# Dummy matmuls from a preset constant and re-queued first loads at the start of an attention-plus-GLU kernel

## The chip, the cores and the metric

The kernel runs on one core of a Trainium2 chip. The time is the device time of one execution in microseconds (us); "span" is the time from the first to the last instruction in the trace, about 1.7 us less. Every kernel here is timed next to the kernel before, on the same chip, in the same rounds.

## The reference

```python
xn = layernorm(x)                                  # x: 1 x 2048 x 512, bf16
q, k, v = split_heads(xn @ wqkv)                   # 32 heads of 16
phi(a) = concat(softmax(a @ w_phi), softmax(-(a @ w_phi)))
o = phi(q) @ (phi(k)^T v) / (phi(q) @ sum(phi(k)) + 1e-6)
out = x + o @ wo + ((xn @ w_gate) * (xn @ w_up)) @ w_down      # inner width 1792
```

Tokens are handled in 16 tiles of 128. What matters here is the start: load x tiles 0 to 3, centre and transpose them, multiply tiles 0 and 1 by the v weights, run the first two gate/up units, then fold `w_phi` into the k weights. From there on TensorE never waits.

## The kernel before

The first loads go out on two queues, SyncE's (SP) and ScalarE's (ACT), in this order (one load fetches one *slice* of a weight matrix, or one or two tiles of x):

```python
    load_x(0, 1)                 # SP : x tile 0, 128 KB
    load_x(1, 1, ACT)            # ACT: x tile 1
    load_v(SP, 0)                # first half of the v weights, 256 KB
    load_v(ACT, 1)               # second half
    load_x(2, 2)                 # tiles 2 and 3, 256 KB
    load_gu(ACT, 0, (0,))        # first gate slice, 256 KB
    load_gu(SP, 0, (1,))         # first up slice
    load_gu(SP, 1)               # next slices
    ...
    dve(lambda e: e.memset(zero, 0.0), [], ["zero"], 256)
```

TensorE's program starts with dummies on those zeros, which only keep the array busy:

```python
    def warm(n, w=512):
        def fn(e):
            ...
            for _ in range(n):
                ins = e.matmul(bank(7, 0, w), lhsT=zero[:, 0:128], rhs=zero[:, 0:w], start=True, stop=True)
            return ins
        sc.step(PE, fn, ["zero"], [("ps", 7)], n * w * 0.8)

    warm(7)
    ...                              # statistics, centring
    x_transpose(0, 2, 0, 2)
    x_transpose(0, 3, 1, 2)
    warm(2, 128)
    v_matmul(0, 0, (0,))
    x_transpose(1, 4, 0, 2, DVE)
    x_transpose(1, 5, 1, 2, DVE)
    v_matmul(0, 0, (1,))
    v_matmul(1, 1)
    ...
    g0a()                            # first halves (256 tokens) of two gate/up units
    g1a()
    x_transpose(2, 2)
    u0a()
    x_transpose(3, 3)
    u1a()
    ...
    g0b()                            # second halves: need tiles 2 and 3
```

Steps of one engine run in program order; a step waits on semaphores for the data that it reads. A load waits for nothing.

The softmax here doesn't subtract the row's maximum and nothing guards it: scores larger than these inputs give would overflow.

## Time and profile before

| | before |
|---|---|
| median, lowest, highest of the first three runs | 222.69, 222.11, 223.19 us |
| span of the profiled run (223.13 us) | 221.4 us |
| TensorE share of the chain that ended last | 96% |
| first real matmul work (transpose of tile 0) | 4.88 us |
| first fold of `w_phi` | 15.50 us |

The first fold is my marker for the whole start, because behind it TensorE runs without a wait: a later fold is a longer run by nearly the same amount (from first fold to the end of the span it is 205.83 to 205.90 us in all fourteen traces).

The timeline of TensorE in the kernel before; the columns are start and duration in us, engine, line, operation, output and input, shape of weights and moving operand, count, and in brackets the idle time before and what ended it. Neighbours of one line are merged, so durations overlap and a line can hold more than one shape.

```profile
1.25 3.17 PE L644 MATMUL ps<-arena 128*128 128x512 bf16 x7 [1.25 <-DVE arena L296]
4.88 0.61 PE L421 MATMUL ps<-arena 128*128 128x128 bf16 x4 [0.47 <-DVE arena L389]
...
5.76 1.04 PE L223 MATMUL ps<-arena 128*128 128x512 bf16 x2
6.59 0.63 PE L421 MATMUL ps<-arena 128*128 128x128 bf16 x4
7.01 3.43 PE L223 MATMUL ps<-arena 128*128 128x512 bf16 x14
10.28 0.39 PE L421 MATMUL ps<-arena 128*128 128x128 bf16 x4
...
12.02 3.65 PE L223 MATMUL ps<-arena 128*128 128x256 bf16 x24 [0.25 <-ACT arena L204]
15.50 0.61 PE L337 MATMUL ps<-arena 128*128 128x128 bf16 x8
```

L644 is the dummies, L421 the transposes, L223 the v and gate/up matmuls, L337 the fold. TensorE idles before the first transpose, and once more before 12.02, where the second halves wait for ScalarE to copy tile 3's transpose out of PSUM, the memory that TensorE writes to. (Matmul ends are modelled. By the starts of the matmuls the second gap is 0.42 us longer than the spacing that they should have.)

How fast the array runs is read from groups by shape. This is the group of the eight v matmuls in 5.5 to 9.45 us of the kernel before (count, busy us, mean ns of one, idle before):

```profile
L223 PE MATMUL ps<-arena 128*128 128x512 bf16 x8 | 3.6, 605 | 0.1
```

One takes 605 ns here and 379 ns in the steady part. Starts of neighbours lie 0.427 us apart up to 9.15 us; afterwards two of 256 columns take 0.218: half rate, then full. I call that change the *release* of the clock; it is at 9.2 here. The loads of ScalarE's queue:

```profile
0.79 1.28 ACT L759 ACT_TABLE_LOAD   x1 [0.79 <-PEq L887]
0.82 0.39 ACTq L249 DMA_DIRECT2D arena<-in_A_x_dram  x1
1.25 0.46 ACTq L260 DMA_DIRECT2D arena<-in_A_wqkv_dram  x1
1.74 0.50 ACTq L260 DMA_DIRECT2D arena<-in_B_w_gate_dram  x1
```

Landings (last of the 16 completion records of each load): tile 0 at 3.57, tile 1 3.73, v halves 5.43 and 5.72, tiles 2/3 7.17, first gate slice 8.56, first up slice 8.78.

### The profile page before, as it was taken

The page shows a single profiled execution, that of the slowest core. Times are in us where ns is not written, and L with a number is a line of the kernel's source. Part 1 is how long each engine was busy: PE and PEld are TensorE (multiplying, and loading weights), DVE is VectorE, ACT ScalarE, POOL GpSimd, SP SyncE. Part 2 cuts the span into 40 slices and gives each one's busy share as a digit, 9 for nine tenths or more (in the row PEclk, how much of TensorE's full clock was granted, in tenths as well). Part 3 has the DMA queues.
Part 4 walks back from the last instruction along what each step waited for, and adds up shares of the span by engine and source line. Part 5 has one row for each costly group of instructions (what it writes and reads, how often), then busy time and mean ns, then how long its engine had stood idle before and what let it go on. Part 6 is the DMA issues. An engine that isn't in the chain of part 4 may idle for free.

```text
span 221.4 us, 3319 instructions
## 1 busy us (share of the span) xinstructions
PE 217.0 (98%) x1275; PEld 105.9 (48%) x1275; DVE 141.5 (64%) x246; ACT 85.8 (39%) x161; POOL 53.4 (24%) x119
## 2 busy tenths in 40 slices
PE   6999999999999999999999999999999999999995
PEld 2565444444444454444444444544445444444453
DVE  3646899887466655674586565697776677545341
ACT  4268964687524543444346435531112221000000
POOL 3030273331222012201232422225342222200000
DMA  5998627299200000000002211244674445352221
GB/s 175 280 313 279 150 94 131 58 291 231 47 3 0 0 0 3 0 0 0 3 0 47 49 25 25 51 82 84 149 159 98 109 105 116 76 118 73 60 63 47
DMA packets 47248, 19.90 MB, mean 90 GB/s; under 512 B 37504, under 2 KB 46720, under 8 KB 47232
## 3 DMA queue, kind: packets, MB, share of 16 engines
q1 hardware_dynamic: 46288, 19.03, 35.3%
q10 hardware_dynamic: 944, 0.66, 0.9%
q8 instruction: 10, 0.16, 0.3%
q14 instruction: 6, 0.05, 0.1%
HBM read 8.67 MB, written 2.10 MB: 49 GB/s over the span
## 4 chain that ended last, share of the span: by engine, by line
PE 96%; DMA 1%; DVE 1%; ACT 0%; issue 0%
PE ps L223 91%; PE ps L543 2%; PE ps L496 2%; DMA arena<-in_A_x_dram 1%; PE ps L337 1%; PE ps L421 1%; ACT arena L204 0%; DVE arena L364 0%; DVE arena L389 0%; DVE arena L625 0%; DVE arena L365 0%
## 5 line engine op out<-in xcount | busy, mean ns | idle before, releaser
L223 PE MATMUL ps<-arena 128*128 128x512 bf16 (+3 forms) x962 | 208.9, 373 | 0.3 <-ACT arena L204 0.3
L223 PEld LDWEIGHTS ps<-arena 128*128 128x128 bf16 x962 | 91.2, 98 | 99.3 <-ACT arena L204 0.8
L204 ACT ACTIVATE arena<-ps 128x512 bf16<-128x512 f32 (+2 forms) x114 | 63.0, 593 | 89.3 <-PE ps L223 74.6
L601 DVE TENSOR_TENSOR arena<-ps,arena 128x512 bf16<-128x512 f32 x56 | 38.5, 687 | 23.3 <-PE ps L223 18.0
L451 DVE TENSOR_REDUCE arena<-arena 128x64 f32<-128x1024 bf16 x32 | 38.5, 1214 | 21.0 <-ACT arena L204 21.0
L461 POOL TENSOR_TENSOR arena<-arena 128x512 bf16<-128x512 bf16 x32 | 33.8, 1056 | 1.3
L459 POOL TENSOR_TENSOR arena<-arena 128x32 f32<-128x32 f32 x32 | 8.5, 267 | 91.2 <-DVE arena L455 50.8
L625 DVE TENSOR_TENSOR arena<-ps,arena 128x512 bf16<-128x512 f32 (+2 forms) x13 | 8.5, 650 | 21.5 <-PE ps L223 21.5
L204 ACT ACTIVATE arena<-arena 128x512 bf16<-128x512 bf16 (+2 forms) x28 | 14.2, 519 | 5.7 <-DMA arena<-in_A_x_dram 2.9
L204 ACT ACTIVATE arena<-ps,arena 128x512 bf16<-128x512 f32 x16 | 10.1, 685 | 5.7 <-PE ps L223 5.7
L364 DVE BATCH_NORM_STATS2 arena<-arena 128x6 f32<-128x512 bf16 x16 | 10.4, 672 | 2.4 <-DMA arena<-in_A_x_dram 2.4
L564 DVE TENSOR_TENSOR arena<-ps,arena 128x512 bf16<-128x512 f32 x16 | 11.1, 691 | 0.5
L484 DVE TENSOR_TENSOR arena<-ps,arena 128x512 bf16<-128x512 f32 x16 | 10.3, 643 | 0.0
L455 DVE RECIPROCAL arena<-arena 128x64 f32<-128x64 f32 x16 | 8.4, 533 | 0.0
L496 PEld LDWEIGHTS ps<-arena 128*128 128x128 bf16 x128 | 6.2, 97 | 3.8
L543 PEld LDWEIGHTS ps<-arena 128*128 128x128 bf16 x128 | 6.2, 97 | 3.8
L401 POOL TENSOR_SCALAR arena<-arena 128x1 f32<-128x1 f32 x12 | 3.0, 265 | 19.1 <-ACT arena L204 19.1
L543 PE MATMUL ps<-arena 128*128 128x68 bf16 x128 | 6.7, 194 | 0.0
L496 PE MATMUL ps<-arena 128*128 128x68 bf16 x128 | 6.7, 194 | 0.0
L563 DVE RECIPROCAL arena<-arena 128x32 f32<-128x32 f32 x16 | 5.7, 353 | 0.6
L457 DVE RECIPROCAL arena<-arena 128x32 f32<-128x32 f32 x16 | 5.4, 344 | 0.2
L478 POOL CAST arena<-arena 128x32 bf16<-128x32 f32 x16 | 5.1, 321 | 0.0
(31 smaller groups left out, 35.1 us busy)
## 6 DMA issues: line engine op xcount, KB each, us to landing
out_dram<-arena SPq DMA_DIRECT2D x15, 128.0 KB, 1.7
arena<-in_B_w_down_dram SPq DMA_DIRECT2D x1, 1792.0 KB, 8.0
arena<-in_A_x_dram SPq DMA_DIRECT2D x3, 512.0 KB, 3.8
arena<-arena SPq DMA_TRANSPOSE x44, 2.6
arena<-in_B_w_gate_dram SPq DMA_DIRECT2D x1, 640.0 KB, 8.4
arena<-in_B_w_up_dram SPq DMA_DIRECT2D x1, 640.0 KB, 9.5
arena<-in_B_w_gate_dram SPq DMA_DIRECT2D x1, 512.0 KB, 5.1
arena<-in_B_w_up_dram SPq DMA_DIRECT2D x1, 512.0 KB, 6.1
```

The lines of the kernel that those rows point to most:

```text
L204: return sc.step(ACT, lambda e: e.activation(out=out_ap, in_=in_ap, func=func, scale=scale, **kw), reads, writes, 130.0 + 0.833 * n)
L223: ins = e.matmul(out_ap, lhsT=l, rhs=r, start=start and i == 0, stop=stop and i == npair - 1, **kw)
L364: dve(lambda e: e.bn_stats(stats_v[:, t, 0:6], x_tile(t)), [("x", t)], [("st", t)], 512)
L451: dve(lambda e: e.tensor_reduce(out=sm, in_=e_v, axis=AX.X, op=ALU.add), [(name, s, 0), (name, s, 1)], [("sums", sr)], 1024)
L459: pool(lambda e: e.tensor_tensor(out=rat, in0=sm[:, :, 0], in1=rs[:, :, 1], op=ALU.mult), [("sums", sr), ("rs", s)], [("rat", s)], 32)
L461: pool(lambda e: e.tensor_tensor(out=e_v[:, :, 1, :], in0=e_v[:, :, 1, :], in1=rat[:, :, None].to_broadcast([128, H, 16]), op=ALU.mult), [ ...
L484: dve(lambda e: e.tensor_tensor(out=vs_tile(t)[:, :, 0:16], in0=bank(b).rearrange("p (h f) -> p h f", h=H), in1=rp.unsqueeze(2).to_broadca ...
L496: ins = e.matmul(bank(c // 4, (c % 4) * CW, CW), lhsT=ek[:, c * 128:(c + 1) * 128], rhs=vs[:, c * CW:(c + 1) * CW], start=(t == 0 and c % ...
L543: ins = e.matmul(bank(b0 + c // 4, (c % 4) * CW, CW), lhsT=ph[:, c, :], rhs=kvz_v[:, c, :], start=True, stop=True)
L564: dve(lambda e: e.tensor_tensor(out=o_tile(t).rearrange("p (b h f) -> p b h f", b=2, f=16), in0=nd[:, :, :, 0:16], in1=w_v[:, r].unsqueeze ...
L601: dve(lambda e: e.tensor_tensor(out=hT_v[:, ft, sg * 512:(sg + 1) * 512], in0=bank(bu), in1=g, op=ALU.mult), [("ps", bu), ("g", s)], [("hT ...
L625: dve(lambda e, ps=ps, stg=stg, cs=cs: e.tensor_tensor(out=stg, in0=ps, in1=x_tile(t)[:, cs], op=ALU.add), [("ps", bk), ("x", t)], [("ostg ...
```

## The change

The intent: (1) dummies on a constant that the framework has already written when the engines are released, so that they start about 0.45 us earlier; (2) tiles 0 and 1 in one load with nothing beside it, because the second queue is to begin only behind ScalarE's table load (a small activation, `pace`, stands ahead of its loads); (3) the transposes of tiles 2 and 3 one gate/up part earlier, so that their copies finish in time. Cut to its core:

```diff
-    load_x(0, 1)
-    load_x(1, 1, ACT)
+    load_x(0, 2)
     load_v(SP, 0)
-    load_v(ACT, 1)
-    load_x(2, 2)
-    load_gu(ACT, 0, (0,))
-    load_gu(SP, 0, (1,))
+    load_v(SP, 1)
+    load_gu(SP, 0, (0,))
+    act(sbf("lnv", 0, 1), eps_f, ["eps"], ["pace"])
+    load_x(2, 2, ACT)
+    load_gu(ACT, 0, (1,))
     load_gu(SP, 1)
...
-    dve(lambda e: e.memset(zero, 0.0), [], ["zero"], 256)
...
-                ins = e.matmul(bank(7, 0, w), lhsT=zero[:, 0:128], rhs=zero[:, 0:w], start=True, stop=True)
+                ins = e.matmul(bank(7, 0, w), lhsT=nc.const_aps.tensor(1.0, (128, 128), BF16),
+                               rhs=nc.const_aps.tensor(1.0, (128, w), BF16), start=True, stop=True)
...
-    warm(7)
+    warm(8)
+    warm(1, 256)
...
-    warm(2, 128)
-    v_matmul(0, 0, (0,))
+    warm(1, 128)
     x_transpose(1, 4, 0, 2, DVE)
     x_transpose(1, 5, 1, 2, DVE)
-    v_matmul(0, 0, (1,))
+    v_matmul(0, 0)
     v_matmul(1, 1)
...
     g0a()
+    x_transpose(2, 2)
     g1a()
-    x_transpose(2, 2)
+    x_transpose(3, 3)
     u0a()
-    x_transpose(3, 3)
     u1a()
```

More of the change, by code (lines that the diff above doesn't have):

```diff
@@ L150, in _build @@
     alloc("ostg", 3 * 512)
-    alloc("zero", 512, at=layout["hT"])
     alloc("wphi", NQ * 16)
@@ L231, in _build @@
     mask = sb("mask", 0, CW)
-    zero = sb("zero", 0, 512)
     eps_f = sbf("eps", 0, 1)
@@ L276, in load_v, with c_fn @@
         load_w(eng, wv_v[:, 2 * h:2 * h + 2, :], i, ("wv", h), 262144)
+    def c_fn(e):
+        e.memset(ident, 0.0)
+        e.memset(mask16, 1.0)
+        return e.memset(mask, 1.0)
+    pool(lambda e: e.memset(eps_f, 1e-5), [], ["eps"], 1)
+    pool(c_fn, [], ["const"], 300)
     sc.pin = True
-    load_x(0, 1)
-    load_x(1, 1, ACT)
+    load_x(0, 2)
     load_v(SP, 0)
-    load_v(ACT, 1)
-    load_x(2, 2)
-    load_gu(ACT, 0, (0,))
-    load_gu(SP, 0, (1,))
+    load_v(SP, 1)
[3 more added lines that the diff above has]
+    load_gu(ACT, 0, (1,))
     load_gu(SP, 1)
@@ L293, in _build @@
     sc.pin = False
-    dve(lambda e: e.memset(zero, 0.0), [], ["zero"], 256)
-    def c_fn(e):
-        e.memset(ident, 0.0)
-        e.memset(mask16, 1.0)
-        e.memset(mask, 1.0)
-        return e.memset(eps_f, 1e-5)
-    pool(c_fn, [], ["const", "eps"], 300)
     def select(ap, op, fill, base, pattern, cm):
@@ L601, in gate @@
         dve(lambda e: e.tensor_tensor(out=hT_v[:, ft, sg * 512:(sg + 1) * 512], in0=bank(bu), in1=g, op=ALU.mult),
-            [("ps", bu), ("g", s)], [("hT", ft, sg)] + (["zero"] if ft == 0 and sg == 0 else []), 512)
+            [("ps", bu), ("g", s)], [("hT", ft, sg)], 512)
         sc.prio = 1
@@ L643, in fn @@
             for _ in range(n):
-                ins = e.matmul(bank(7, 0, w), lhsT=zero[:, 0:128], rhs=zero[:, 0:w], start=True, stop=True)
-            return ins
-        sc.step(PE, fn, ["zero"], [("ps", 7)], n * w * 0.8)
-    warm(7)
+                ins = e.matmul(bank(7, 0, w), lhsT=nc.const_aps.tensor(1.0, (128, 128), BF16),
+                               rhs=nc.const_aps.tensor(1.0, (128, w), BF16), start=True, stop=True)
+            return ins
+        sc.step(PE, fn, [], [("ps", 7)], n * w * 0.8)
+    warm(8)
+    warm(1, 256)
     sc.pin = True
```

## The prediction

> **What bounds the kernel now.** TensorE. The chain of waits gives PE 96% of the 221.4 us span and shows no PE wait after 12.02 us. The change leaves that part alone. Only the first 12 us can move. The timeline of that stretch shows:
>
> - Dummies run 1.25 to 4.42 us, behind the DVE memset of their zeros. The engines are released at 0.79.
> - x tile 0 lands at 3.57, tile 1 at 3.73 (two 128 KB loads, issued at 0.80 and 0.82). Statistics 0.70, aggregation 0.18 and centring 0.29 put the first transpose at 4.88: 1.31 us after landing. TensorE idles 4.42 to 4.88.
> - Matmuls start 0.427 us apart for 512 columns until about 9.2 us, 0.218 after it: half clock until then. All eight v matmuls (4.88 to 9.4, with transposes) run slow.
> - The third and fourth transposes are at 10.28 and 10.94, and the second half of the GLU waits from 11.6 to 12.02 for ScalarE to copy the last one out.
>
> The Trainium skill ("TensorE: Matmul & The Clock Gate", Part 1) says the array starts at half rate and is released after about 3.4 us sustained activity, by a free-running window. The trace fits: windows 5.8 to 9.2 (busy) and 2.4 to 5.8 (holding the 0.46 us gap, not released).
>
> **What the change does.**
> 1. Dummies from about 0.80: eight of 0.427 plus one of 0.213 end near 4.43, as before, but last 3.6 us instead of 3.0.
> 2. One 256 KB load for tiles 0 and 1. Data moved at about 290 KB/us from 2 us on. If the second queue starts late, as intended, I estimate landing near 3.2, first transpose near 4.5, no gap: activity is unbroken from 0.8, and full clock could come between 4.2 and 7.6 instead of 9.2.
> 3. Transposes of tiles 2 and 3 move up by one GLU part each: the 0.42 us wait goes.
> 4. Gate/up slices land at an estimated 7 to 8 (8.56, 8.78 before).
>
> Up to the second GLU half there are about 4.45 us of full-clock work. With first transpose S and clock release F it ends at S + 4.45 + (F - S)/2. S 4.5, F 5.8 gives 9.6; F 7.6 gives 10.5; F unchanged 11.3; before 12.02. Then slice landings and the fold's transposed weights (13.03; the fold began at 15.66) cap the gain near 2.5 us.
>
> **Doubt.** The ScalarE operation meant to hold back its DMA may not do it. In the trace ScalarE's DMA issue at 0.824 passes the table load running 0.79 to 2.08; a queued activation whose semaphore is satisfied may be passed too. Then tiles 2/3 are issued near 1.0, compete with tiles 0/1, the first transpose is near 5.1, the gap stays, and only the 0.4 us of item 3 is won. I give this 45%.
>
> **Prediction.** 221.3 us, 80% range 220.2 to 222.6. Faster by over 2%: 0.02; within 2%: 0.97; slower: 0.01.
>
> **Right or wrong in the profile.** Dummy start 0.8; ScalarE's first DMA issue 2.1 or later (held) or near 1.0 (not); tile 0/1 landing near 3.2; first transpose 4.5; spacing change from 0.427 to 0.218 before 7.6; no ScalarE wait before the second half; first fold near 13.2 to 14.5.
>
> **What would make it wrong.** The free-running phase of the clock window (the three runs spread 1.1 us already); queue passing as above; v weights or the first gate slice landing later than the v work ends; transposes not counting as activity.

## The result, and the profile after

| | before | after |
|---|---|---|
| median of six runs (us) | 222.30 | 221.61 |
| lowest to highest | 221.69 to 223.19 | 221.51 to 221.96 |
| ratio | | 0.997 (95%: 0.9946 to 0.9994) |
| span of the profiled run | 221.4 | 220.2 |
| first transpose | 4.88 | 5.19 |
| first fold | 15.50 | 14.40 |

A ratio is the mean time of one kernel's runs over that of the other's of the same rounds, so it is not quite the ratio of the medians. The gain is 0.7 us, a third of a per cent. Both profiled runs are slow ones of their kernel (223.13 and 221.96 us).

The timeline of TensorE in the kernel after (L640 dummies, L417 transposes, L222 v and gate/up, L333 the fold):

```profile
0.83 3.79 PE L640 MATMUL ps<-const-bfloat16-1.0 128*128 128x512 bf16 x9 [0.83 <-PEq L884]
5.19 0.48 PE L417 MATMUL ps<-arena 128*128 128x128 bf16 x4 [0.57 <-DVE arena L385]
...
5.58 0.48 PE L417 MATMUL ps<-arena 128*128 128x128 bf16 x4
6.04 0.60 PE L222 MATMUL ps<-arena 128*128 128x512 bf16 x2
7.44 1.89 PE L222 MATMUL ps<-arena 128*128 128x512 bf16 x10 [0.80 <-DMA arena<-in_A_wqkv_dram]
9.17 0.39 PE L417 MATMUL ps<-arena 128*128 128x128 bf16 x4
...
10.06 4.51 PE L222 MATMUL ps<-arena 128*128 128x256 bf16 x32
14.40 0.61 PE L333 MATMUL ps<-arena 128*128 128x128 bf16 x8
```

The v matmuls of the kernel after, by shape, in 5.2 to 8.75 us:

```profile
L222 PE MATMUL ps<-arena 128*128 128x512 bf16 x8 | 2.1, 380 | 0.8 <-DMA arena<-in_A_wqkv_dram 0.8
```

Three things are to be seen. All eight v matmuls now run at full rate (380 ns); the spacing changes at about 5.4 us, among the first transposes, and the clock record of this trace has the release at 5.41. The first transpose is 0.31 us later, not earlier. And TensorE now waits in the middle of the v work for v weights, a wait that the kernel before did not have. The wait before the second halves is gone.

ScalarE and its queue in the kernel after explain the second and third:

```profile
0.79 1.28 ACT L756 ACT_TABLE_LOAD   x1 [0.79 <-PEq L884]
0.93 0.38 ACTq L247 DMA_DIRECT2D arena<-in_A_x_dram  x1
1.34 0.45 ACTq L258 DMA_DIRECT2D arena<-in_B_w_up_dram  x1
2.09 0.20 ACT L203 ACTIVATE arena<-arena 128x1 f32<-128x1 f32 x1
```

The load of tiles 2/3 was issued at 0.93, the first up slice at 1.34; the activation that should hold them back ran at 2.09, behind the table load. The hold does not hold. So these 512 KB travel next to tiles 0/1 and the v weights. Tiles 0/1 land at 3.88 (3.57 and 3.73 before), tiles 2/3 at 4.67 and the up slice at 6.50, long before their use, and the second v half at 7.31 (5.72 before). The chain of waits of the kernel after says the same; its columns are start and length of each piece:

```profile
1.71 5.60 DMA arena<-in_A_wqkv_dram
7.31 0.14 issue
7.44 1.89 PE ps L222 x10
```

Summed up from the two traces, in terms that end at the first fold: the first transpose 0.31 us later; time lost to half rate 2.1 us less (from 4.88 to 9.2 before, which costs half of that, 2.16; about 0.1 after); the wait for v weights 0.96 more (from 6.48, when the next matmul was due, to 7.44); the wait for ScalarE's copies 0.42 less; one short dummy less, 0.06. That makes 1.3 less. Measured is 1.10; the rest, 0.2, is small waits around the transposes that this sum does not split.

### The profile page after: what moved, and what is told of

The parts are those of the page before. It is cut to its first block, busy times and chain, and to the rows that moved or that the text cites. A ratio compares the mean times of both kernels' runs of the same rounds, so it can differ in the third digit from the quotient of the medians.

```text
span 220.2 us, 3319 instructions
## 1 busy us (share of the span) xinstructions
PE 215.7 (98%) x1276; PEld 105.3 (48%) x1276; DVE 141.2 (64%) x245; ACT 85.9 (39%) x162; POOL 53.4 (24%) x119
## 4 chain that ended last, share of the span: by engine, by line
PE 96%; DMA 3%; SPq 0%; issue 0%; DVE 0%
PE ps L222 91%; DMA arena<-in_A_wqkv_dram 3%; PE ps L539 2%; PE ps L492 2%; PE ps L333 1%; PE ps L417 0%; SPq L258 0%; SPq L247 0%; DVE arena L621 0%
## 5 line engine op out<-in xcount | busy, mean ns | idle before, releaser
L222 PE MATMUL ps<-arena 128*128 128x512 bf16 (+3 forms) x962 | 207.2, 371 | 0.8 <-DMA arena<-in_A_wqkv_dram 0.8
L222 PEld LDWEIGHTS ps<-arena 128*128 128x128 bf16 x962 | 90.8, 98 | 99.2 <-ACT arena L203 1.3
L203 ACT ACTIVATE arena<-arena 128x512 bf16<-128x512 bf16 (+3 forms) x29 | 14.4, 508 | 4.5 <-POOL arena L397 2.6
L550 POOL TENSOR_SCALAR arena<-arena 128x32 f32<-128x32 f32 x4 | 1.2, 291 | 16.3 <-DVE arena L447 16.3
```

The source lines that it names most:

```text
L203: return sc.step(ACT, lambda e: e.activation(out=out_ap, in_=in_ap, func=func, scale=scale, **kw), reads, writes, 130.0 + 0.833 * n)
L222: ins = e.matmul(out_ap, lhsT=l, rhs=r, start=start and i == 0, stop=stop and i == npair - 1, **kw)
```

## The experiments

Two questions are open after the two traces.

First, is the gain the clock or the loads? Theory 1: the earlier, longer dummies release the clock earlier, and the new loads cost time. Theory 2: the loads and the moved transposes are the gain, and the release falls where it falls. From experiment 5 on the first half of theory 1 has a sharper form, theory W: the release comes at the end of a free-running window (that of the page which the prediction names) that a short gap does not spoil, and a late load can hide a late release.

Second, would the change have gained more, had its hold worked? Theory H says that the loads of the second queue stand in the way of the v weights. Its rival says that only the total of bytes counts, so that any order ends in the same wait.

Each kernel below was correct. "First fold" is from the timeline of its own trace, the release of the clock is from the clock record of that trace, or, where there is none (the kernel before in both its traces, experiments 1, 5 and 6), an estimate from the spacing of the instruction starts.

### 1. The dummies alone

```diff
 # kernel before
-    dve(lambda e: e.memset(zero, 0.0), [], ["zero"], 256)
-    warm(7)                      # on zeros
+    warm(8)                      # on the preset constant
+    warm(1, 256)
```

> The kernel before with one part of the change alone: the dummies read the preset constant, start with the engines' release and last 3.6 us. Loads, their order and the transposes are as before. Theory 1 (the change's gain is an earlier clock release; its loads cost time): the spacing of 512-column matmuls changes from 0.427 to about 0.216 us before 6 us, v work is done near 7.5, TensorE then waits for the first gate slice (near 8.6) and for the copies of tiles 2 and 3; first fold near 14.7 (15.50 in the trace of before), time 221.5 to 222.0 with a narrow spread. Theory 2 (the gain is the loads and the moved transposes; the release falls where a free-running window puts it): release still near 9, first fold near 15.5, about 222.3 with a spread over 1 us.

Measured: 221.77 us (221.44 to 223.02), ratio 0.9975 (0.9938 to 1.0013). Release at 4.9; TensorE waits for the first gate slice, which lands at 8.26, and for ScalarE's copies; first fold 14.41, the very place where the kernel after has it. In the trace this is theory 1; but the old dummies can give an early release as well (experiments 6 and 12), so one trace does not show that the new ones caused it. The narrow spread that it expected did not come: one of six runs took 223.02. The interval includes 1, so the ratio alone proves nothing.

### 2. The change without its dummies

```diff
 # kernel after
-    warm(8)                      # on the preset constant
-    warm(1, 256)
+    dve(lambda e: e.memset(zero, 0.0), [], ["zero"], 256)
+    warm(7)                      # on zeros
```

> The kernel after with the old dummies: seven, on zeros that VectorE writes first, start at 1.25 us; loads and transposes as after. Theory 1: the release comes late (8 to 9.5 us) as in the trace of before, the v work runs at half clock, first fold near 15.0 (14.40 after), 221.9 to 222.4. Theory 2: like the kernel after, 221.6, first fold 14.4.

Measured: 221.81 us (221.58 to 222.92), ratio 0.9981 (0.9944 to 1.0018); first fold 14.23. Theory 2's numbers are the nearer ones, but not for its reason. Two lines of the timeline:

```profile
5.96 0.81 PE L223 MATMUL ps<-arena 128*128 128x512 bf16 x2
7.27 1.89 PE L223 MATMUL ps<-arena 128*128 128x512 bf16 x10 [0.50 <-DMA arena<-in_A_wqkv_dram]
```

The release came at 6.38, 1 us later than in the kernel after (5.41): the first two v matmuls still start 0.427 us apart, at 5.96 and 6.39. Then TensorE stands idle until the second v half has landed at 7.14, so the late release only shortened that wait and cost nothing. With experiment 1 this says that the parts do not add up: each alone gives about what both give together (both intervals include 1), because the wait for the v weights hides what a late release would cost.

### 3. The hold made real

```diff
 # kernel after: the load waits on a semaphore that the activation sets
-    load_x(2, 2, ACT)
+    load_x(2, 2, ACT, ["pace"])
```

> The kernel after with the hold of the second queue made real: its load of tiles 2 and 3 waits for a semaphore that the small activation sets. Theory H (tiles 2/3 and the first up slice, issued at 0.93 and 1.34, pushed the second half of the v weights to 7.31 and held tiles 0/1 back): ScalarE's first DMA issue near 2.4, tiles 0/1 land by 3.5 (3.88 after), the second v half by 5.8, first transpose by 4.8 (5.19), no wait for v weights (0.80), first fold 13.2 to 13.8 (14.40), 220.6 to 221.1. Rival (the transfers are limited by total bytes, the order only moves the wait to the first gate and up slices): the same time as after, 221.6, with the wait before the GLU parts.

Measured: 222.55 us (221.99 to 223.15), ratio 1.0003 (0.9967 to 1.0039). Half of theory H came true: first issue at 2.31, tiles 0/1 at 3.48, second v half at 5.43, first transpose at 4.80, no wait for v weights. But its time is wrong. The timeline of its TensorE:

```profile
4.80 0.61 PE L417 MATMUL ps<-arena 128*128 128x128 bf16 x4 [0.19 <-DVE arena L385]
...
8.39 0.61 PE L222 MATMUL ps<-arena 128*128 128x256 bf16 x4 [0.56 <-DMA arena<-in_B_w_gate_dram]
...
11.00 3.23 PE L222 MATMUL ps<-arena 128*128 128x256 bf16 x25 [0.94 <-DMA arena<-in_B_w_up_dram]
```

The wait moved, as the rival said, and grew. The held queue now has the first up slice second in line; issued at 2.74, it lands at 10.95, while the next gate slice, issued at 2.72 on the other queue and needed later, takes its share of the engines and lands at 10.09. First fold 15.36. Holding a queue back does not make the other's data come first where it matters, if needed data sits in the held queue.

### 4. One queue, in the order of use

```diff
 # kernel after
     load_x(0, 2)
     load_v(SP, 0)
     load_v(SP, 1)
-    load_gu(SP, 0, (0,))
-    act(sbf("lnv", 0, 1), eps_f, ["eps"], ["pace"])
-    load_x(2, 2, ACT)
-    load_gu(ACT, 0, (1,))
+    load_x(2, 2)
+    load_gu(SP, 0)
```

> The kernel after with all early loads on SyncE's queue in the order of use: tiles 0/1, v weights, tiles 2/3, first gate, first up slice; no small activation. Theory H: like the real hold, 220.6 to 221.1; the first v half cannot be overtaken, tiles 0/1 land by 3.5. Rival (two queues are needed to fill the 16 engines early): tiles 0/1 land no earlier than 3.88, or later slices come over 0.5 us later than with the real hold; 221.5 or more.

Measured: 221.02 us (220.77 to 221.35), ratio 0.9937 (0.9900 to 0.9973), the best here and clear of 1. Its TensorE:

```profile
4.86 0.61 PE L415 MATMUL ps<-arena 128*128 128x128 bf16 x4 [0.26 <-DVE arena L383]
...
5.80 2.49 PE L222 MATMUL ps<-arena 128*128 128x512 bf16 x12
8.12 0.39 PE L415 MATMUL ps<-arena 128*128 128x128 bf16 x4
...
9.00 4.51 PE L222 MATMUL ps<-arena 128*128 128x256 bf16 x31
13.35 0.61 PE L331 MATMUL ps<-arena 128*128 128x128 bf16 x8
```

No wait for a load is left behind the first transpose. Tiles 0/1 land at 3.55, the v halves at 4.31 and 5.01, the gate slice at 7.20, the up slice at 8.09. The rival falls: one queue is not slower at the start. This agrees with what the Trainium skill says ("DMA: Bandwidth & Descriptors", "Issuing engines are not separate DMA queues"): all queues feed the same 16 engines and interleave, and issuing from several "will only save the time on the sequencer". Here that saving was worth less than the order: in all four traces with one queue (experiments 4, 5, 7 and 10) the loads landed in the order of issue. The runs do not separate one queue from the order of use, though: the loads of the kernel before, in nearly that order on two queues, were not tried with the new dummies and the moved transposes together.

### 5. One queue with the old dummies

The loads of experiment 4 with the dummies of experiment 2.

> The one-queue kernel with the old dummies (zeros, start 1.25 us). With its loads no wait for data is left before the first fold, so nothing hides the half-clock time any more. Theory W (the clock is released at the end of a free-running window of about 3.4 us after the dummies start; a late load hides a late release): release anywhere from 4.7 to 9.2 us, so the time spreads over 0.8 us or more and its median is 0.3 to 0.8 above the one-queue kernel's 221.0. Rival (the dummies' start does not matter, a gap is what delays): the gap before the first transpose is longer than in the one-queue kernel, so always late: release after 8, first fold near 14.6, 222.0 or more in every run. If the dummies are worth nothing: 221.0 with the narrow spread of the one-queue kernel.

Measured: 221.39 us (220.97 to 221.69), ratio 0.9955 (0.9917 to 0.9993). The release is near 7.3 (an estimate: two v matmuls start 0.394 us apart, at 6.93 and 7.32, between 0.427 and 0.216) and first fold 13.86, so half rate is paid for in the open now; the median is 0.37 above experiment 4's (another chip, so only roughly). The spread, 0.72, is a little less than theory W said. The rival, a late release in every run, falls.

### 6. The moved transposes alone

```diff
 # kernel before
     g0a()
+    x_transpose(2, 2)
     g1a()
-    x_transpose(2, 2)
+    x_transpose(3, 3)
     u0a()
-    x_transpose(3, 3)
     u1a()
```

> The kernel before with the transposes of tiles 2 and 3 moved up by one GLU part each, nothing else. If the 0.42 us wait for ScalarE's copies is on the path: gone, first fold up to 0.4 earlier for the same release time, 222.0. Rival (the wait is only exchanged for the first gate or up slice or for tiles 2/3's centring): same as before within 0.2, about 222.3.

Measured: 222.05 us (221.51 to 222.77), ratio 0.9986 (0.9949 to 1.0023). The wait for the copies is gone from the trace. The release happened to come before the first transpose at 4.90 (the spacing is that of full rate from there on), and TensorE then waited for the first gate slice, which landed at 8.92 here; first fold 14.64. What the move alone is worth is below what these runs can show.

### 7. One queue, the gap filled with dummies

```diff
 # experiment 4
-    warm(8)
-    warm(1, 256)
+    warm(9)
+    warm(1, 128)
```

> The one-queue kernel with its dummies prolonged to 4.77 us, so that no gap is left before the first transpose at 4.86. Theory W (a window with a gap of half a microsecond still releases the clock): same, 221.0, same spread. Rival (unbroken activity matters): release by 4.9 in the trace and in most runs, 220.5 to 220.8, narrower spread. Both lose up to 0.1 if the dummies overrun the first transpose.

Measured: 221.54 us (221.08 to 222.18), ratio 0.9964 (0.9928 to 1.0001). No gain, but it is also slower than theory W said. The trace has the release at 4.85, as the rival said, and a wait of 0.66 us for the gate slice, which landed at 7.92 instead of 7.20; first fold 13.64. The load's landing, not the clock, set this one, so its time decides between neither: the rival's early release is there, its gain is not.

### 8 and 11. The kernel after, twice more

> The kernel after, unchanged, on the same chip as the three runs beside it. Theory W: the wait for the second v half hides any release up to about 7.5 us, so the spread stays below 0.6 us and the median 221.6; the release in the trace lies at another time than 5.3. Rival (the release has a fixed place after the dummies' start): again at 5.3.

> The kernel after, unchanged, as the partner of the one-queue kernel: 221.6, the second v half lands near 7, first fold 14.0 to 14.4, a spread below 0.6 apart from a stray run.

Measured: 221.58 us (five runs in 221.53 to 221.62, one at 223.64), ratio 0.998 (0.9938 to 1.0023), and 221.76 us (five runs in 221.61 to 221.98, one at 223.68), ratio 0.9977 (0.9932 to 1.0022). The release is at 6.05 in one trace and at 4.81, before the first transpose, in the other, so it has no fixed place. The second v half lands at 6.88 and 7.10, first fold 13.97 and 14.19. The two stray runs near 223.7 fit neither theory's words. Their results list a granted clock of 0.992, every other run of this kernel 1.000: 0.8% of 221.9 us, 1.8 us of clock lost, is most of the 2 us by which they are longer. So the strays too are mostly a matter of the clock; no trace of such a run was taken, and why they lost it stays open.

### 9. The change without the small activation

> The kernel after without the small activation. If the activation holds nothing back, its removal changes nothing but the issue of ScalarE's first load, 0.93 to about 0.82: tiles 0/1 land near 3.8, the second v half near 7, first fold 14.0 to 14.4, 221.5. If the activation did hold something, the second v half comes later by several tenths.

221.32 us; first issue of ScalarE's queue at 0.81 instead of 0.93; tiles 0/1 at 4.07, second v half at 6.63, first fold 13.73. The activation delays the issue by 0.1 us and not until it has run. This fits an issue that waits until the activation's own input is there: in the trace of after GpSimd writes that input from 0.79 to 0.89, and the issue follows at 0.93. The fold came earlier than I expected, since the v half did; a single look does not say that the activation does harm.

### 10. One queue again, beside the kernel after

> The one-queue kernel again, now on the same chip as the kernel after. If its lead is real: 221.0 to 221.4, lower than the kernel after beside it by 0.2 to 0.6, first fold before 14.0. If the first time was luck of the chip: within 0.1 of the kernel after.

Measured: 221.27 us (220.48 to 222.00), ratio 0.9938 (0.9902 to 0.9974), next to 221.76 and 0.9977 of the kernel after on the same chip. Its lead on the medians is 0.49, and the ratio to the kernel before is that of experiment 4 again. The expectation for the trace failed: first fold 14.14, because the gate slice landed at 8.42 in the profiled run (222.0 us, the slowest of the six), and TensorE waited for it.

### 12. The kernel before

> The kernel before, unchanged, for a second trace. If the release is a lottery of the window's phase, it lies elsewhere than 9.2 (4.7 to 8.1 by the window's length), and the first fold comes earlier with it, by up to 0.9 us, until the landing of the first gate slice (near 8.6) caps it. If it has a fixed place, again 9.2 and first fold 15.5.

Measured: 221.36 us, faster than any of the 18 runs of the kernel after. Its TensorE, to be held against the first trace of the same kernel:

```profile
1.24 3.04 PE L644 MATMUL ps<-arena 128*128 128x512 bf16 x7 [1.24 <-DVE arena L296]
4.85 0.48 PE L421 MATMUL ps<-arena 128*128 128x128 bf16 x4 [0.57 <-DVE arena L389]
...
5.69 0.59 PE L223 MATMUL ps<-arena 128*128 128x512 bf16 x2 [0.25 <-ACT arena L204]
...
10.26 3.65 PE L223 MATMUL ps<-arena 128*128 128x256 bf16 x24 [0.25 <-ACT arena L204]
13.74 0.61 PE L337 MATMUL ps<-arena 128*128 128x128 bf16 x8
```

Its v matmuls by shape, in 5.5 to 9.45 us:

```profile
L223 PE MATMUL ps<-arena 128*128 128x512 bf16 x8 | 2.1, 380 | 0.2 <-ACT arena L204 0.2
```

The same program, first transpose at the same place (4.85), but 380 ns instead of 605: the clock was released before the first transpose, not at 9.2. The four transposes, too, take 0.48 us instead of 0.61, and the dummies 3.04 instead of 3.17, because the last one is shorter (0.50 us instead of 0.63). Where a clock record exists, a matmul shortened like that is the one in which the release falls (0.54 and 0.59 in experiments 4 and 2, released 0.31 and 0.42 after its start), so I estimate the release here near 4.0. That is earlier than the 4.7 to 8.1 that I expected, and the fold moved more than the 0.9 us that I allowed. First fold 13.74 instead of 15.50, 1.76 us earlier; the span is 219.6 instead of 221.4, the same 1.76 by the unrounded spans (221.39 and 219.64). An earlier first gate slice (7.50 instead of 8.56) let the early release take effect. This pair is the clearest evidence: what moved the kernel before from one run to the other is when the clock was released and when the gate slice landed.

### What the traces say together

Set the first fold against the landing of the load that TensorE waited for:

| trace | load | landed | first fold | difference |
|---|---|---|---|---|
| after | second v half | 7.31 | 14.40 | 7.09 |
| 8 | second v half | 6.88 | 13.97 | 7.09 |
| 11 | second v half | 7.10 | 14.19 | 7.09 |
| 9 (no activation) | second v half | 6.63 | 13.73 | 7.10 |
| 2 (old dummies) | second v half | 7.14 | 14.23 | 7.09 |
| 6 (moved only) | first gate slice | 8.92 | 14.64 | 5.72 |
| 7 (filled) | first gate slice | 7.92 | 13.64 | 5.72 |
| 10 (one queue) | first gate slice | 8.42 | 14.14 | 5.72 |

With the change's loads the second v half decides, to 0.01 us, whatever the dummies are and whenever the clock was released (4.81 to 6.38 in these five). With the other orders it can be the first gate slice. In experiments 4 and 5 it was neither: there the clock and the work itself set the fold (13.35 and 13.86).

All runs of the two kernels and of the one-queue version:

| | runs | median | lowest to highest | over 222.5 us |
|---|---|---|---|---|
| before | 40 | 222.37 | 221.29 to 223.72 | 17 |
| after | 18 | 221.63 | 221.51 to 223.68 | 2 |
| one queue (4 and 10) | 12 | 221.12 | 220.48 to 222.00 | 0 |

They come from several chips, so the table shows shapes, not exact differences.

## Why the prediction was right or wrong

**The number.** 221.3 was predicted with 220.2 to 222.6; 221.61 was measured. That is inside, and "within 2%" was right. The first fold, 14.40, also lay inside the forecast 13.2 to 14.5. But terms of the sum were wrong and offset each other, so that the number came out so near is partly luck.

**TensorE bounds the kernel and only the start can move.** Right: behind the first fold the two traces run alike (spans differ by 1.15 us, folds by 1.10).

**"Dummies from about 0.80" and "the 0.42 us wait goes".** Both right: 0.83, and no wait for ScalarE before the second halves.

**"If the second queue starts late, as intended".** The favoured case, given 55%, did not happen. The doubt did: the queued activation was passed, tiles 2/3 were issued at 0.93, the first transpose came at 5.19 (5.1 said). The trace of before carried the hint, a load issued at 0.82 during the table load. The Trainium skill ("Perfetto Trace Analysis", "Per-engine timelines", "DVE / Act Engine Instruction") draws it the same way: the sequencer pushes an activation into a queue and is then ready for the next instruction. Here the issue at 0.93 against the activation at 2.09 agrees.

**"The gap stays, and only the 0.4 us of item 3 is won."** This step failed. The gap did stay (0.57 us in the profile), yet the clock was released at 5.41, 0.2 us behind it. I had read one trace of before, with a release at 9.2, as what a gap does. Experiment 2 has the old dummies, a gap of 0.62 us from 4.41 and a release at 6.38, experiment 8 a gap of 0.49 us and a release at 6.05. So a gap of about half a microsecond does not forbid an early release. (In experiments 12 and 6 the release came before the gap was over, so they say nothing of it.) The same failed step left out a cost: in that case the v weights come late, 0.96 us of new wait. I had listed it among what would make the prediction wrong, not in the sum. The two errors, about 2 us of clock and 1 us of wait, partly offset.

**The favoured case would have failed as well.** "Gate/up slices land at an estimated 7 to 8" held only if both slices had their turn. With a real hold (experiment 3) they landed at 8.34 and 10.95, and the first fold at 15.36 instead of 13.2 to 14.5.

**What the gain is.** In the traces, the clock. With the new dummies the release lay between 4.8 and 6.2 us in all nine traces that have them; with the old ones near 4.0, between 4.2 and 4.9, at 6.38, near 7.3, and at 9.2. The Trainium skill ("TensorE: Matmul & The Clock Gate", "What's actually happening") has a free-running window of 3.4 us. From dummies at 0.83 the end of the first whole window lies between 4.2 and 7.7, and all nine fit; from 1.24 it lies between 4.7 and 8.1, and of the five 6.38 and 7.3 fit and the one between 4.2 and 4.9 may. The 4.0 is too early for a whole window and the 9.2 too late, and why stays open. (One thing speaks for a fixed step: in all nine traces with a clock record the stretch at full rate lasts 215.04 us, which is 63 times 3.413, wherever it begins.) That the earlier start narrows the release is thus likely, not proven, by five traces against nine; nor were start, length and operand of the dummies (ones in place of zeros) varied one at a time. And in the kernel after, a release at 6.38 costs nothing anyway, because TensorE waits for v weights until 7.0 or later in its three traces (experiment 2 and the table of landings). This fits that its runs, two strays apart, lie within 0.5 us, and also that none of them is as fast as a lucky run of the kernel before: the change trades a lottery for a wait of 0.5 to 1.0 us (its three traces). With all loads on one queue in the order of use, the wait for the v weights is gone; what can take its place is a wait for the first gate slice (0.66 and 1.07 us in experiments 7 and 10).

## What to carry to other kernels

Before believing a cause at the start of a kernel, take a second trace of the same kernel: here two traces of one program differ by more than twice what the change gained. Try issuing loads in the order of their use on one queue: it gave the two best medians here. An operation placed ahead of a load did not hold it back here (issue at 0.93, operation at 2.09) until the load waited for its semaphore (2.31), and then whatever else was in that queue was held too. And a wait that hides another cost makes two improvements look alike and not add up, so try them on a version without that wait.

## What the Trainium skill lacked or had wrong

- "TensorE: Matmul & The Clock Gate", table of the two states: full rate after a busy window of about 3.4 us "sustained". The kernel after was released at 5.41 with a gap of 0.57 us in the 3.4 us before, the second trace of before near 4.0 (an estimate), 2.8 us after its dummies began at 1.24. The page does not say how much idleness a window may hold, nor what explains a release at 9.2 with dummies from 1.25.
- The same page, Part 4: transposes take about 275 ns in a kernel and full rate "doesn't engage" for them. Here the starts of neighbouring transposes lie 0.107 us apart before the release and 0.056 after, as for any 128-column matmul (the modelled duration of one falls from 314 to 219 ns).
- The same page, Part 1: the ramp is under 1% of a typical span and not worth fitting. The size agrees (1.76 us of 221, with a part from the gate slice), but it is more than twice what this change gained, and most of the 2.4 us between the fastest and the slowest run of the kernel before (221.29 and 223.72).
- "Perfetto Trace Analysis", "DVE / Act Engine Instruction": it does not say which later instructions of the sequencer may pass a queued activation. Here a load issue came at 0.93 (0.81 without the activation), just after the activation's input was written (0.89), and did not wait for its execution (2.09).
- "DMA: Bandwidth & Descriptors": it says that DMAs from several engines interleave, but gives no figure for what a second queue does to the landing of the first one's data. Here 512 KB on the second queue moved the landing of the second v half from 5.0 to 5.5 us (four traces with one queue) to 6.6 to 7.3 (five traces with two).
